# Turning the key-value sums over DRAM instead of on TensorE, normalising both query heads on ScalarE, and a new order of work

## The chip, the core and the metric

The kernel runs on one core of one Trainium2 chip. A core has five engines that run side by side and wait for each other by semaphores: TensorE (PE in the profile; PEld is its loading of weights), VectorE (DVE), ScalarE (ACT), GpSimd (POOL), and SyncE (SP), which here only issues DMAs. The time is that of one execution on the device in microseconds. A version is judged by the median of several runs; for the kernel before that is 1006.31 us over three runs, which lie between 1004.87 and 1006.49 us.

## The reference

Two stages. First linear attention over 8 batches of 8 heads, 576 tokens a batch, head size D = 64, with M = 128 random features:

```
phi(x) = exp(h - max(h)) / sqrt(M),  h = x @ omega.T - sum(x*x)/2      (x scaled by D**-0.25)
kv  = sum over s of phi(k)[s, m] * v[s, d]        # per batch and head: M x D
z   = sum over s of phi(k)[s, m]                  # per batch and head: M
out = (phi(q) @ kv) / (phi(q) @ z + 1e-6)
```

Then, over all 4608 tokens with the 8 heads side by side (512 columns), a feed-forward layer: `h = x @ w_in` (512 by 2048), `g = h - tanh(h)`, `g @ w_out` (2048 by 512). All inputs and the output are float32.

## The kernel before

**Precision by pieces.** TensorE works on float32r operands here. Where a product has to be better than one such pass, an operand is split into a high part (the cast) and a low part (the difference), and the product is the sum of two or three matmuls. ScalarE makes the high parts, VectorE (or GpSimd) the low ones.

**Units.** Work is cut into units, each with short steps. `f{ch}{f}` is one of 9 x 16 feed-forward units: token chunk `ch` (512 tokens) and block `f` (128 of the 2048 columns). Its steps are `h0` to `h3` (12 matmuls of 512 columns, L945), `th` (tanh on ScalarE, L974), `g` (VectorE, L975), `gh` and `gl` (high part on ScalarE, L963; low part on VectorE, L977), and `o0` to `o3` (12 matmuls, L970 to L972). `k{b}{c}` holds the keys and values of batch `b` and head pair `c`; `q{ch}{c}` the queries of chunk `ch` and head pair `c`. The first two batches and the first chunk use simpler native units (`k0*`, `k1*`, `n**`), and the weights are decoded during the first 120 us or so (`d*`).

**A query unit.** Features are made in `phi_q` (projection, L690, L695, exponent L701). VectorE forms the denominators (L732) and their reciprocals (L737, step `rc`). Steps `n0` and `n1` multiply the features of the two heads by them: `QN = "VA"` puts head 0 on VectorE in one instruction (L742) and head 1 on ScalarE in four (L745). Step `z` turns the features in blocks of 32 by 32 on VectorE (L750), step `s` writes them to DRAM with four DMAs (L756), step `r` reads them back into the layout that TensorE wants (L760). Steps `a`, `l`, `m` split them (L770, L774) and multiply them by the key-value sums (L780, L781); `ta` and `tv` bring the result to `xs` (L784, L788).

**A key unit.** Its matmuls (L852) gather in one PSUM bank, `pk`, for both heads: on the 128 partitions lie the 64 columns of the values' high parts and the 64 of their low parts, and along the row the 128 features, once for the keys' high and once for their low parts. Step `ca` (ScalarE, L879) and `cv` (VectorE, L882) add the two key parts into `c`, a tile of 128 x 2 heads x 128. Then step `kt` works on TensorE: two transposes of 128 x 128 (L886), one for each head, and one matmul that spreads the sums `z` over all partitions (L887). After that the value parts lie side by side; `ka` copies one of them (ScalarE, L892) and `kb` adds the other (VectorE, L895), which gives `kvt`; `zb` copies the spread `z` (L899); `wa` and `wv` split `kvt` into the operand `kvw` (L904, L907) that the query units use. The sums `z` themselves are made on GpSimd (L859, L860, L864) in a small tile `zs`, which is a part of `zf` (columns 14 and 15), and folded on VectorE (L867).

**Order.** The order of all steps is written out by hand in the string `ORDER`, some 4,900 words such as `k51.kt` or `f46.h0.5` (unit, step, and PSUM bank or buffer). The program issues the steps in this order, each to its own engine; every engine works off its instructions strictly in that order, and waits where an operand isn't ready. So an instruction that waits holds back everything behind it on its engine. The DMAs of SP form one such queue too. Matmuls of the feed-forward units fill TensorE while the attention units pass through the other engines.

Of the kernel before, what the change touches and what calls it, by code (L numbers as in the profile page):

```python
# [1088 lines left out]
```

## Time and profile before

| | us |
|---|---|
| median of three runs (lowest to highest) | 1006.31 (1004.87 to 1006.49) |
| the profiled execution, its own time | 1005.32 |
| span in its profile, first to last instruction | 1003.5 |
| TensorE busy | 986.4 (98% of the span) |
| VectorE busy | 802.9 (80%) |
| ScalarE busy | 683.4 (68%) |
| GpSimd busy | 325.3 (32%) |

A row of a group of instructions has the line, the engine and operation, what is written and read, the shape, the count, the busy time, the mean duration of one, and the idle time of the engine just before them with what ended it. Matmuls overlap: one may start while another is still running through, so the step from start to start tells what one costs in a row of them, and the duration of one doesn't. A wait row says who waited for whom, the sum in us, how often, and the longest.

### The profile page before, as it was taken

The numbers are of one execution on the slowest core, as the hardware profiler recorded it, in microseconds if no ns is written. First come the engines' busy times: TensorE is split into PE (matmuls) and PEld (weight loads), VectorE is DVE, ScalarE is ACT, GpSimd is POOL, SyncE is SP. The second block draws the span as 40 slices with busy tenths as digits, with TensorE's granted clock in tenths as the row PEclk, the third lists the DMA queues.
The fourth block names the chain that finished last, engine by engine and source line by source line (L and its number), as shares of the span: only waits on it lengthen the run. The fifth ranks groups of instructions, "written<-read, shape, count | busy, mean of one in ns | idle before, by whom it ended". The sixth has DMA issues, their size and how long they took to land.

```text
span 1003.5 us, 16665 instructions
## 1 busy us (share of the span) xinstructions
PE 986.4 (98%) x5024; PEld 817.8 (81%) x5024; DVE 802.9 (80%) x2698; ACT 683.4 (68%) x1677; POOL 325.3 (32%) x561
## 2 busy tenths in 40 slices
PE   9999999999999999999999999999999999999998
PEld 8688778888788788888888877888888888888886
DVE  7899868888888998988889999889999866744222
ACT  7878877677775787777767787687777675643222
POOL 2334314434334436343353434453623410001000
PEclk9899999999999999999999999999999999999999
DMA  9944731222302331312423222314222223110001
GB/s 356 374 165 77 178 88 56 82 82 65 108 20 80 99 108 57 101 53 75 129 56 98 77 86 71 101 30 117 66 77 71 69 85 105 32 54 32 1 10 43
DMA packets 45034, 91.15 MB, mean 91 GB/s; under 512 B 4880, under 2 KB 21648, under 8 KB 42896
## 3 DMA queue, kind: packets, MB, share of 16 engines
q1 hardware_dynamic: 43072, 84.12, 26.7%
q0 software_dynamic: 1584, 5.77, 3.0%
q8 instruction: 40, 0.66, 0.3%
q14 instruction: 50, 0.41, 0.1%
q10 hardware_dynamic: 288, 0.20, 0.1%
HBM read 60.18 MB, written 24.12 MB: 84 GB/s over the span
## 4 chain that ended last, share of the span: by engine, by line
PE 74%; DVE 14%; ACT 5%; DMA 3%; issue 2%; SPq 0%; POOL 0%; ACTq 0%; DVEq 0%; POOLq 0%
PE h L945 31%; PE po L970 10%; PE po L972 10%; PE po L971 10%; PE pj_q L684 2%; PE pk_k L852 2%; PE pn_q L781 1%; DMA phi_q<-qd_q 1%; DVE zf L975 1%; DVE zr L977 1%; DVE zf L732 1%; DVE qq_q L774 1%; PE pn_q L780 1%; DMA w<-a 1%; PE pj_k_B L684 1%
## 5 line engine op out<-in xcount | busy, mean ns | idle before, releaser
L945 PE MATMUL h<-xa,w 128*128 128x512 f32 x1728 | 439.6, 391 | 2.7 <-DMA w<-a 1.7
L945 PEld LDWEIGHTS h<-xa,w 128*128 128x128 f32 x1728 | 317.4, 188 | 68.7 <-DMA w<-a 2.1
L970 PE MATMUL po<-w,zr 128*128 128x512 f32 x576 | 226.8, 394 | 0.1
L972 PE MATMUL po<-w,zr 128*128 128x512 f32 x576 | 224.9, 390 | 0.3 <-DVE zr L977 0.3
L971 PE MATMUL po<-w,zr 128*128 128x512 f32 x576 | 224.8, 390 | 0.0
L977 DVE TENSOR_TENSOR zr<-zf,zr 128x512 fp32r<-128x512 f32 x144 | 103.1, 716 | 63.6 <-ACT zr L963 62.0
L963 ACT CAST zr<-zf 128x512 fp32r<-128x512 f32 x144 | 89.5, 621 | 88.5 <-PE po L971 48.3
L974 ACT ACTIVATE zf<-h 128x512 f32<-128x512 f32 x144 | 85.9, 597 | 76.2 <-PE h L945 49.8
L975 DVE TENSOR_TENSOR zf<-h,zf 128x512 f32<-128x512 f32 x144 | 98.7, 685 | 48.8 <-ACT zf L974 47.3
L972 PEld LDWEIGHTS po<-w,zr 128*128 128x128 f32 x576 | 108.1, 188 | 24.8 <-DVE zr L977 1.1
L970 PEld LDWEIGHTS po<-w,zr 128*128 128x128 f32 x576 | 108.2, 188 | 22.0 <-issue 1.3
L971 PEld LDWEIGHTS po<-w,zr 128*128 128x128 f32 x576 | 108.2, 188 | 19.1
L701 ACT ACTIVATE phi_q<-phi_q,nb_q 128x128 f32<-128x128 f32 x224 | 76.1, 397 | 4.2 <-DVE nb_q L695 3.9
L932 POOL TENSOR_TENSOR xa<-xs,xa 128x512 fp32r<-128x512 f32 x16 | 23.0, 1441 | 168.4 <-DVE xs L788 103.9
L824 POOL TENSOR_TENSOR khl_k_A<-phi_Ak,khl_k_A 128x256 fp32r<-128x256 f32 x48 | 38.8, 811 | 106.6 <-DVE khl_k_A L820 104.4
L732 DVE CUSTOM_DVE_ANT_0 zf<-phi_q,zb_k 128x128 bf16<-128x128 f32 (+1 forms) x240 | 63.4, 300 | 2.7 <-ACT zb_k L899 0.8
L695 DVE CUSTOM_DVE_ANT_0 phi_q<-pj_q,phi_q 128x128 f32<-128x128 f32 x224 | 54.5, 283 | 8.9 <-ACT phi_q L690 8.4
L774 DVE TENSOR_TENSOR qq_q<-phi_q,qq_q 128x512 fp32r<-128x512 f32 x56 | 41.6, 743 | 20.0 <-ACT qq_q L770 19.7
L824 POOL TENSOR_TENSOR khl_k_B<-phi_Bk,khl_k_B 128x256 fp32r<-128x256 f32 x48 | 38.9, 816 | 41.0 <-DVE khl_k_B L820 37.4
L690 ACT COPY phi_q<-pj_q 128x256 f32<-128x256 f32 x112 | 39.4, 370 | 18.8 <-PE pj_q L684 18.2
L770 ACT CAST qq_q<-phi_q 128x512 fp32r<-128x512 f32 x56 | 34.6, 617 | 22.6 <-PE pn_q L781 11.9
L684 PE MATMUL pj_q<-om,x_q 128*128 128x256 f32 x224 | 42.4, 288 | 1.8 <-DVE xs L788 0.9
(151 smaller groups left out, 1686.9 us busy)
## 6 DMA issues: line engine op xcount, KB each, us to landing
raw<-w SPq DMA_DIRECT2D x16, 1024.0 KB, 9.3
qd_q<-tq_q SPq DMA_DIRECT2D x112, 128.0 KB, 2.4
phi_q<-qd_q SPq DMA_DIRECT2D x28, 512.0 KB, 3.4
out<-zf SPq DMA_DIRECT2D x35, 256.0 KB, 2.0
f_q<-qT SPq DMA_DIRECT2D x28, 256.0 KB, 3.0
v_k<-vt SPq DMA_DIRECT2D x24, 288.0 KB, 2.8
f_k<-kT SPq DMA_DIRECT2D x24, 288.0 KB, 3.2
w<-a POOLq DMA_DIRECT2D x11, 512.0 KB, 4.6
```

The source lines that it names most:

```text
L684: nc.tensor.matmul(v["pj"][:, i], x, om2, start=True, stop=True)
L701: nc.scalar.activation(u[kind][:, at + i], u[kind][:, at + i], AF.Exp, bias=v["nb"][:, i : i + 1], scale=-1.0)
L732: nc.vector.tensor_tensor_reduce(next(turn)[r], u["ph"][r, i], kvs[b, c][1][r, h], scale=1.0, scalar=EPS, op0=ALU.mult, op1=ALU.add, accum ...
L824: nc.gpsimd.tensor_sub(k[:, :m, 1], u["ph" + g[0]][:, t : t + m], k[:, :m, 0].bitcast(F32))
L945: nc.tensor.matmul(u["p"], w_, x[:, c], start=(c, i) == (0, 0), stop=(c, i) == (NC - 1, 2))
L963: nc.scalar.copy(u["gh"], g)
L970: nc.tensor.matmul(po, gh, whi, start=f == 0, stop=False)
L971: nc.tensor.matmul(po, gh, wlo, start=False, stop=False)
L972: nc.tensor.matmul(po, gl, whi, start=False, stop=f == NF - 1)
L974: st = dict(th=lambda: nc.scalar.activation(g, blocks(u["p"]), AF.Tanh), g=lambda: nc.vector.tensor_sub(g, blocks(u["p"]), g), gh=g_hi, gl ...
L975: g=lambda: nc.vector.tensor_sub(g, blocks(u["p"]), g),
L977: gl=lambda: nc.vector.tensor_sub(u["gl"], g, u["gh"].bitcast(F32)))
```

## The change

In the key unit the two transposes on TensorE, the copy `ka` and the addition `kb` are gone. In their place VectorE folds the lower 64 partitions of `c` onto the upper 64 (`cf`), turns the 64 x 256 result in blocks of 32 by 32 (`ct`), writing into `zs`; SP writes it to DRAM with two DMAs (`cs`), and reads it back into `kvt` with one (`kb`, now a DMA). `kt` keeps the matmul for `z` alone. `wa` and `wv` read and write the same elements in another pattern. `QN` becomes `"AA"`: ScalarE normalises both heads, with eight instructions, and VectorE none. The string `ORDER` is new as a whole.

```diff
-QN = "VA"
+QN = "AA"
...
-k51.zh.1 k51.ca f46.h2 k52.vhA0.0 f45.gh.1 k51.cv k51.zl f46.h3 q51.e3 q50.r f45.gl q51.e2 k51.kt f47.h0.2 k52.sv1
-k51.zb f46.th f47.h1 q51.d3 k51.ka k51.kb f47.h2 q51.d2 k51.wa f47.h3 k52.vlA0 q51.rc q50.a0 k52.vlA1 f45.o0 f46.g
...
+k51.kt f46.h3 k51.zb k51.cf f47.h0.5 k51.ct f46.th q51.d2 k51.cs f47.h1 f46.g s3.d2 f47.h2 k52.vlA0 f46.gh.0 f47.h3
+q51.d3 k52.vlA1 q50.a0 q51.rc f48.h0.6 f46.gl q51.n1 f48.h1 q50.l0 k51.kb f45.o0 k52.tA0 q51.n0 k52.sv1 q50.m0.7 f45.o1
+q50.ta0 q51.z f45.o2 k52.eA0 f48.h2 k51.wa q52.sv k52.cA1 q51.s f47.th f46.o0 f45.o3 f47.g f48.h3 q53.ld k52.khA0.0
...
-        def turned():
-            for h in range(2):
-                nc.tensor.transpose(u["pk"][:, 0, h], u["c"][:, h], ident)
+        def c_fold():
+            nc.vector.tensor_add(u["c"][0:D], u["c"][0:D], u["c"][D:P])
+
+        def c_turned():
+            nc.vector.transpose(zs[0:D].rearrange("p h m -> p (h m)").rearrange("p (j h c) -> p h j c", j=4, h=2),
+                                u["c"][0:D].rearrange("p h (j c) -> p h j c", c=32))
+
+        def c_scatter():
+            d = u["d"] = dr.tile([4, 32, 2, D], F32, tag="cd", name=f"cd_{n}", bufs=2)
+            for i in range(2):
+                nc.sync.dma_start(d[:, :, i].rearrange("j r x -> r j x"),
+                                  zs[32 * i : 32 * i + 32].rearrange("p h m -> p (h m)").rearrange("p (j x) -> p j x", j=4))
+
+        def c_gather():
+            y = ak.tile([P, 2, 2, 32], F32, tag="kvt", name=f"kvt_{n}")
+            nc.sync.dma_start(y.rearrange("p i h c -> p (i h c)"), u["d"].rearrange("j r i x -> (j r) (i x)"))
+            u["kvt"] = y.rearrange("p i h c -> p h i c")
+
+        def z_all():
             nc.tensor.matmul(u["pk"][:, 1].rearrange("p h m -> p (h m)"), ones[:, 0:1].to_broadcast([P, P]),
                              u["zhl"][:, 0].rearrange("p h m -> p (h m)"), start=True, stop=True)
-
-        def kv_hi():
-            u["kvt"] = ak.tile([P, 2, D], F32, tag="kvt", name=f"kvt_{n}")
-            nc.scalar.copy(u["kvt"], u["pk"][:, 0, :, D:])
-
-        def kv_sum():
-            nc.vector.tensor_add(u["kvt"], u["pk"][:, 0, :, 0:D], u["kvt"])
...
+        def w_part(s):
+            return u["w"][:, s, :].rearrange("p h (i c) -> p h i c", c=32)
+
         def w_hi():
             u["w"] = sb.tile([P, 4, D], F32R, tag=f"kvw{b % 2}{c}", name=f"kvw_{n}")
-            nc.scalar.copy(u["w"][:, 0::3, :], u["kvt"])
+            nc.scalar.copy(w_part(slice(0, 4, 3)), u["kvt"])
 
         def w_lo():
-            nc.vector.tensor_sub(u["w"][:, 1:3, :], u["kvt"], u["w"][:, 0::3, :].bitcast(F32))
+            nc.vector.tensor_sub(w_part(slice(1, 3)), u["kvt"], w_part(slice(0, 4, 3)).bitcast(F32))
```

How the new order moves instructions is shown at the end of one key unit, batch 5 and head pair 1 (`k5_1`). TensorE before, from the last matmuls of that unit's sums on; `pk_k5_1` is its PSUM bank, `pj_k5_2` the projection of the next key unit, `h_4_6` and `po_4_0` feed-forward work:

```order
L852 MATMUL pk_k5_1_6135<-khl_k5_1_B0_6234,vhl_k5_1_B0_6191 128x256 x2
L852 MATMUL pk_k5_1_6135<-khl_k5_1_B1_6275,vhl_k5_1_B1_6198 128x256 x2
L684 MATMUL pj_k5_2_A0_6311<-om_93,x_k5_2_6256 128x256 x2
L945 MATMUL h_4_6_6292<-xa_98,w6_951 128x512 x6
L886 MATMUL pk_k5_1_6135<-zf_70,c1_k5_1_6316 128x128 x2
L887 MATMUL pk_k5_1_6135<-zhl_k5_1_6314,ones_96 128x256
L945 MATMUL h_4_7_6338<-xa_98,w7_917 128x512 x12
```

And TensorE now, around the same unit's matmul for `z`:

```order
L985 MATMUL po_4_3_6103<-w4_871,zr_69 128x512
L986 MATMUL po_4_3_6103<-w4_871,zr_69 128x512
L987 MATMUL po_4_3_6103<-w4_871,zr_69 128x512
L687 MATMUL pj_k5_2_A1_6396<-om_93,x_k5_2_6323 128x256 x2
L906 MATMUL pk_k5_1_6177<-zhl_k5_1_6378,ones_96 128x256
L960 MATMUL h_4_6_6334<-xa_98,w6_956 128x512 x3
L960 MATMUL h_4_7_6407<-xa_98,w7_924 128x512 x12
```

The two transposes are gone; the matmul for `z` remains, and feed-forward work follows it as before.

ScalarE before, from the copy `zb` of that unit past its cast `wa` (`kvw_k5_1`); `dn_q5_1` marks the normalising of the query unit of chunk 5 and head pair 1:

```order
L899 COPY zb_k5_1_6343<-pk_k5_1_6135 128x256
L974 ACTIVATE zf_70<-h_4_6_6292 128x512
L892 COPY kvt_k5_1_6351<-pk_k5_1_6135 128x128
L904 CAST kvw_k5_1_6361<-kvt_k5_1_6351 128x2x64
L770 CAST qq_q5_0_0_6368<-phi_q5_0_5854 128x512
L745 ACTIVATE phi_q5_1_6133<-phi_q5_1_6133,dn_q5_1_6212 128x128 x4
L963 CAST zr_69<-zf_70 128x512
```

And ScalarE now, the same stretch:

```order
L911 COPY zb_k5_1_6404<-pk_k5_1_6177 128x256
L989 ACTIVATE zf_70<-h_4_6_6334 128x512
L978 CAST zr_69<-zf_70 128x512
L773 CAST qq_q5_0_0_6436<-phi_q5_0_5871 128x512
L748 ACTIVATE phi_q5_1_6191<-phi_q5_1_6191,dn_q5_1_6250 128x128 x8
L787 COPY xs_99<-pn_q5_0_0_6465 64x512
L704 ACTIVATE phi_Ak5_2_6384<-phi_Ak5_2_6384,nb_k5_2_A0_6457 128x128 x2
L919 CAST kvw_k5_1_6485<-kvt_k5_1_6452 128x2x64
L693 COPY phi_Ak5_2_6384<-pj_k5_2_A1_6396 128x256
L989 ACTIVATE zf_70<-h_4_7_6407 128x512
L978 CAST zr_69<-zf_70 128x512
```

The copy into `kvt` is gone, the normalising has eight instructions in place of four, and the cast `wa` stands seven rows behind `zb` instead of three, with a projection's copy, a feed-forward tanh and a feed-forward cast right behind it.

SP now, around the same unit; `cd` is the DRAM buffer of the key-value sums, `qd` that of the queries, `f_` and `v_` are loads:

```order
L897 DMA cd_k5_1_6417<-zf_70 32x4x64 x2
L1026 DMA out<-zf_70 128x512
L902 DMA kvt_k5_1_6452<-cd_k5_1_6417 128x128
L759 DMA qd_q5_1_6490<-tq_q5_1_6474 32x4x256 x4
L716 DMA f_q5_3_6506<-qT 128x512
L810 DMA f_k5_3_6511<-kT 128x576
L763 DMA phi_q5_1_6191<-qd_q5_1_6490 128x1024
```

And SP before, in the same place, where the key unit issues nothing:

```order
L811 DMA v_k5_1_6012<-vt 128x576
L713 DMA f_q5_2_6042<-qT 128x512
L811 DMA v_k5_2_6237<-vt 128x576
L756 DMA qd_q5_0_6277<-tq_q5_0_6259 32x4x256 x4
L760 DMA phi_q5_0_5854<-qd_q5_0_6277 128x1024
L756 DMA qd_q5_1_6413<-tq_q5_1_6402 32x4x256 x4
```

Three DMAs of the key unit now stand in SP's queue; the read-back waits there for the two writes to land, and the queries' scatter stands behind it.

## Rows read from the trace of the kernel before

**Rows 1.** The page's list of engines: busy time, share of the span, instructions.

```profile
PE 986.4 (98%) x5024; PEld 817.8 (81%) x5024; DVE 802.9 (80%) x2698; ACT 683.4 (68%) x1677; POOL 325.3 (32%) x561
```

**Rows 2.** Busy time of each engine in five stretches of the span (us from its start: length, then busy time and instructions of each engine, the granted TensorE clock, the DMA share, GB/s).

```profile
0.00:120.00 120.00, 114.13 (x776) 92.55 (x776) 103.75 (x258) 97.57 (x229) 39.76 (x54) 0.97 0.73 241
120.00:300.00 180.00, 178.22 (x898) 146.97 (x898) 151.68 (x537) 130.11 (x328) 66.46 (x121) 1.00 0.25 69
300.00:800.00 500.00, 494.62 (x2460) 413.15 (x2458) 450.32 (x1649) 369.89 (x940) 212.59 (x383) 1.00 0.28 82
800.00:950.00 150.00, 150.00 (x678) 124.63 (x677) 82.97 (x235) 73.25 (x160) 6.54 (x4) 1.00 0.17 52
950.00:1003.50 53.50, 49.41 (x218) 40.53 (x217) 14.18 (x21) 12.54 (x21) 0.00 (x0) 0.99 0.07 25
```

**Rows 3.** TensorE's instructions in order of time, in a row of feed-forward matmuls and where one key unit ends (start, length, engine, line, operation, count).

```profile
401.34 2.88 PE L945 MATMUL h<-xa,w 128*128 128x512 f32 x12
404.06 0.52 PE L684 MATMUL pj_q<-om,x_q 128*128 128x256 f32 x3
...
415.98 0.40 PE L684 MATMUL pj_k_A<-om,x_k 128*128 128x256 f32 x2
416.22 0.38 PE L886 MATMUL pk_k<-zf,c_k 128*128 128x128 f32 x2
416.36 0.36 PE L887 MATMUL pk_k<-zhl_k,ones 128*128 128x256 f32 x1
416.56 0.40 PE L684 MATMUL pj_k_A<-om,x_k 128*128 128x256 f32 x2
```

**Rows 4.** The page's chain of work that ended last, by engine.

```profile
PE 74%; DVE 14%; ACT 5%; DMA 3%; issue 2%; SPq 0%; POOL 0%; ACTq 0%; DVEq 0%; POOLq 0%
```

**Rows 5.** Groups of instructions by line and shape: those that go, those that come more often, and those that stand nearest to the new ones.

```profile
L886 PE MATMUL pk_k<-zf,c_k 128*128 128x128 f32 x48 | 9.1, 271 | 0.0
L886 PEld LDWEIGHTS pk_k<-zf,c_k 128*128 128x128 f32 x48 | 6.4, 139 | 2.5 <-DVE c_k L882 0.2
L892 ACT COPY kvt_k<-pk_k 128x128 f32<-128x128 f32 x24 | 6.5, 269 | 2.1 <-PE pk_k L887 2.1
L895 DVE TENSOR_TENSOR kvt_k<-pk_k,kvt_k 128x128 f32<-128x128 f32 x24 | 6.8, 285 | 0.2
L867 DVE TENSOR_TENSOR zf<-zf 64x256 f32<-64x256 f32 x24 | 10.7, 446 | 2.9 <-POOL zf L864 2.2
L872 DVE CAST zhl_k<-zf 64x256 fp32r<-64x256 f32 x24 | 6.8, 282 | 1.6 <-PE pk_k L852 1.0
L750 DVE STREAM_TRANSPOSE tq_q<-phi_q 128x512 f32<-128x512 f32 x56 | 36.4, 688 | 0.5
L742 DVE TENSOR_TENSOR phi_q<-phi_q,dn_q 128x512 f32<-128x512 f32 x28 | 20.0, 714 | 0.4
L745 ACT ACTIVATE phi_q<-phi_q,dn_q 128x128 f32<-128x128 f32 x112 | 35.8, 391 | 10.6 <-DVE dn_q L737 10.6
```

**Rows 6.** DMAs that the query units send over DRAM: the page's list of issues (count, KB each, median us from issue to landing), and the lengths of the issues on SP (least, median, longest in ns).

```profile
qd_q<-tq_q SPq DMA_DIRECT2D x112, 128.0 KB, 2.4
phi_q<-qd_q SPq DMA_DIRECT2D x28, 512.0 KB, 3.4
L756 SPq DMA_DIRECT2D qd_q<-tq_q x112: 303/437/459, 182.2 to 879.7; - x112
L760 SPq DMA_DIRECT2D phi_q<-qd_q x28: 320/338/338, 186.2 to 882.2; - x28
```

**Rows 7.** Who waited for whom: what ScalarE waited for from those DMAs, and ScalarE's two longest waits in sum.

```profile
ACT qq_q L770 <- DMA qd_q<-tq_q: 5.6, 4, 2.1
ACT qq_q L770 <- DMA phi_q<-qd_q: 4.8, 7, 1.1
ACT zf L974 <- PE h L945: 49.8, 39, 4.4
ACT zr L963 <- PE po L971: 48.3, 20, 6.0
```

**Rows 8.** The same for TensorE, its two longest waits in sum, and for SP's queue, the longest in sum.

```profile
PE h L945 <- DMA w<-a: 1.7, 1, 1.7
PE pn_q L781 <- DVE qq_q L774: 1.4, 4, 0.7
SPq L756 <- DVE tq_q L750: 171.9, 19, 20.3
```

More of the change, by code (lines that the diff above doesn't have):

```diff
@@ new lines @@
+k43.ct k43.cs f3f.h0.7 q50.sa q43.z f3f.h1 s2.d2 k51.ld f3d.gh.1 f3c.o1 q43.s f3d.gl f3f.h2 q50.sv f3f.h3 f3e.th x4.h1
+f3c.o2 k50.lv q42.ta1 f3c.o3 f3e.g q51.ld x4.h0 k43.kb q42.tv1 f3d.o0 f3e.gh.0 x4.l0 f3d.o1 x4.h2 q43.r f3e.gl f3d.o2
+x4.l1 f3f.th k50.pA0.6 k50.vhM.1 k50.pA1.3 k50.cA0 k50.pM.0 f3e.o0 k43.wa k50.cM k50.vhA0.0 k50.cA1 f3e.o1 k50.tM x4.l2
+f3f.g f3e.o2 k50.tA1 q43.a0 k43.wv f3d.o3 k50.tA0 k50.eA1 q43.l0 f3e.o3 f3f.gh.1 k50.vlA0 q50.p0.0.0 q43.m0.7 k50.eA0
+f3f.gl f40.h0.3 q43.a1 k50.khA0.0 k50.klA0 f3f.o0 q50.c0 q43.l1 q43.ta0 f3f.o1 k50.zA s3.c0.1 q43.tv0 q50.p2.6 s3.d0
@@ new lines @@
+q43.m1.4 q50.c2 s3.c1.0 k50.kvA0.7 q43.ta1 f3f.o2 k50.khA1.1 k50.vhA1.0 s3.d1 q43.tv1 f3f.o3 k50.klA1 q50.t0 x4.h3
+f40.h1 k50.vlA1 k50.vlM q50.e0 q50.p3.1 x4.l3 k50.pB0.4 q50.c3 k50.pB1.0 k50.eM k50.kvA1 f40.h2 k50.cB0 k50.cB1 q50.d0
+f40.h3 s3.c2.1 k50.khM.0 s3.c3.0 f41.h0.5 k50.klM f40.th k50.tB0 k50.vhB0.0 s3.d3 k50.kvM k51.sa f40.g q50.p1.2
+k50.vhB1.1 f41.h1 k50.tB1 f41.h2 f40.gh.0 k51.sv0 f41.h3 k50.eB0 f40.gl f42.h0.4 q50.c1 q51.sa k50.khB0.1 k51.sv1 f42.h1
+k50.klB0 f42.h2 k50.vlB0 k50.eB1 f42.h3 f41.th k50.khB1.0 k50.zB q50.t1 f40.o0.3 q50.t3 f40.o1.0 f41.g k50.klB1 q50.t2
@@ new lines @@
+f40.o2.2 f41.gh.1 k50.vlB1 k50.zM k51.pA0.1 k51.lv f41.gl k50.kvB0 k51.cA0 k50.kvB1 k52.ld k51.pA1.5 f43.h0.6 k51.tA0
+k51.cA1 f42.th k50.zf f41.o0 k50.ca k50.zh.1 q50.e1 f42.g f41.o1 k50.zl q50.e2 k50.cv f43.h1 q51.sv k51.vhA0.0 q50.e3
+f40.o3.1 k51.vhA1.1 f41.o2 f42.gh.0 k50.cf f43.h2 k51.eA0 f42.gl k51.pM.4 k50.kt f43.h3 k51.vlA0 k50.zb k51.khA0.0
+k51.cM k50.ct f42.o0 k51.klA0 f43.th k51.tA1 k50.cs k51.tM f42.o1 k51.vlA1 k51.eM q50.d2 q52.ld k51.eA1 f42.o2 q50.d3
+f44.h0.7 k51.khA1.1 q50.d1 f41.o3 f43.g k51.kvA0.5 k50.kb k51.zA q51.p0.4.1 q51.p1.6 q51.c0 f44.h1 f43.gh.1 q51.t0
@@ new lines @@
+k51.klA1 f44.h2 q51.c1 k51.khM.0 q51.e0 k51.vhM.0 f44.h3 f43.gl q51.t1 f42.o3 f44.th q50.rc k51.klM k51.pB0.4 f44.g
+k51.pB1.6 k51.cB0 k51.kvA1 k50.wa f43.o0 k51.tB0 k51.cB1 k51.vhB0.1 f44.gh.0 q51.d0 f45.h0.7 k51.eB0 k51.vlM f45.h1
+k51.vlB0 q51.e1 k50.wv k51.tB1 f45.h2 q50.n0 f44.gl k51.kvM q51.p2.4 k51.khB0.1 k51.vhB1.0 q51.d1 q51.p3.6 q51.c2 f44.o0
+k51.klB0 k51.eB1 f43.o1 q51.c3 k51.zB q50.n1 q51.t3 f44.o1 k51.vlB1 f43.o2 k52.lv k52.sa q50.z k51.zM f45.h3 f46.h0.6
+f45.th f43.o3 k51.khB1.0 q52.sa q50.s f44.o2 k52.sv0 k51.klB1 f46.h1 f45.g k51.kvB0 k51.zf f45.gh.1 k52.pA0.7 k52.vhA0.1
@@ new lines @@
+q51.t2 k51.kvB1 f46.h2 k51.zh.1 k51.ca k52.vhA1.0 k52.cA0 k51.cv k51.zl f44.o3 q51.e2 f45.gl q51.e3 k52.pA1.4 q50.r
+k51.kt f46.h3 k51.zb k51.cf f47.h0.5 k51.ct f46.th q51.d2 k51.cs f47.h1 f46.g s3.d2 f47.h2 k52.vlA0 f46.gh.0 f47.h3
+q51.d3 k52.vlA1 q50.a0 q51.rc f48.h0.6 f46.gl q51.n1 f48.h1 q50.l0 k51.kb f45.o0 k52.tA0 q51.n0 k52.sv1 q50.m0.7 f45.o1
+q50.ta0 q51.z f45.o2 k52.eA0 f48.h2 k51.wa q52.sv k52.cA1 q51.s f47.th f46.o0 f45.o3 f47.g f48.h3 q53.ld k52.khA0.0
+f47.gh.1 k53.ld k51.wv k52.klA0 f46.o1 k52.tA1 f47.gl k52.eA1 f46.o2 k52.khA1.1 k52.kvA0.5 k52.zA f48.th q50.tv0
@@ L921, in k_unit @@
             st["kv" + g] = partial(kv, g=g)
-        st.update(zA=partial(zsum, 0), zB=partial(zsum, 1), zM=z_mid, zf=z_fold, zh=z_hi, zl=z_lo, ca=c_hi, cv=c_sum, kt=turned,
-                  ka=kv_hi, kb=kv_sum, zb=zb, wa=w_hi, wv=w_lo)
+        st.update(zA=partial(zsum, 0), zB=partial(zsum, 1), zM=z_mid, zf=z_fold, zh=z_hi, zl=z_lo, ca=c_hi, cv=c_sum, cf=c_fold, ct=c_turned, cs=c_scatter,
+                  kb=c_gather, kt=z_all, zb=zb, wa=w_hi, wv=w_lo)
         return st
```

622 lines of the change are left out of this document (301 added, 321 removed).

## The prediction

> **What bounds the kernel now.** I read the list of engines first: TensorE is busy for 986.4 of 1003.5 us, VectorE for 80%, ScalarE for 68% [rows 1]. The stretches come next, because an average hides the stage: from 300 to 800 us TensorE has 494.6 of 500 us, VectorE 450.3, ScalarE 369.9; from 800 to 950 us TensorE is never idle, and the others are half free [rows 2]. The granted clock is 1.00 from 120 to 950 us, which is the upper of its two levels. So TensorE sets the pace, and VectorE, at 90%, is the helper with the least room. TensorE's idle time is 5.9 us up to 120, then 1.8, 5.4 and 0.0 up to 950, and 4.1 at the end [rows 2]; its longest wait in sum is one of 1.7 us, the next 1.4 us in four [rows 8]. Busy time is not all work at full pace, since matmuls overlap and their ends are modelled, so short stalls can hide in it; I allow as much again as the 7.2 us that show between 120 and 950. The chain of work that ended last gives TensorE 74% and VectorE 14% [rows 4]: on most of the way a microsecond of matmuls is a microsecond of time, on a quarter of it another engine hands on.
>
> **The change part by part.** All terms are held against the profiled execution, 1005.3 us by its own clock, of which 1003.5 us are its span; it is 1.0 us below the median of 1006.31, inside the spread of the runs.
>
> *The transposes go from TensorE.* The two of one unit start at 416.22 us and the next matmul at 416.36 us, without a gap: 0.14 us for a unit, though the row gives each 271 ns of length [rows 3, 5]. With 24 units that is 3.4 us. Lower bound: only the chain's TensorE share counts, 74% of it, 2.5 us [rows 4]. Upper bound: if the loading of their weights is what really holds the array, 6.4 us [rows 5]. I take 3.3 us, a touch under the full sum, because the start-to-start step is the nearest row and TensorE isn't idle before any of them (0.0 in the row).
>
> The Trainium skill weighs this choice the other way: "VectorE: DVE Perf Modes", section "Rules for kernel authors", says to do a 128 x 128 transpose on TensorE where a PSUM destination will do, and to use VectorE for 32 x 32 blocks. By that rule the step would stay, and the 3.3 us with it. The row decides here, I think, because the rule compares lengths of one operation and this kernel is short of TensorE steps.
>
> *VectorE.* It loses 28 multiplications of 714 ns (20.0 us) and 24 additions (6.8 us). It gains 24 folds of 64 x 256, the form of L867 with 446 ns, 10.7 us, and 24 block transposes of 64 x 256 [rows 5]. The trace has none of that size; L750 takes 688 ns for twice the row, and L872 reads and writes a 64 x 256 tile in 282 ns, so it lies between 6.8 and 16.5 us in sum; I take 350 ns, half of L750, 8.4 us. Net: 7.7 us less (0 to 9).
>
> *ScalarE.* It loses 24 copies (6.5 us) and gains 112 multiplications, at L745's busy time of 35.8 us for as many: 29.3 us more, nearly all from 180 to 880 us. That lifts it from 74% to some 78% there, still under VectorE's 89%. By itself this costs nothing: its two longest waits, 98 us in sum, are for TensorE [rows 7], and in that time the extra work fits. The cover would be gone where a normalising of 8 x 0.32 = 2.6 us stands ahead of a tanh or cast that TensorE wants next; if that held TensorE for 1 us in one of four units, it would be 7 us, the upper bound; the lower is 0. The new order keeps more work between the reciprocal and the turning than before, so I take 0.
>
> *The DRAM trip.* Two writes issue for 0.44 us each and land after 2.4 us, the read issues for 0.34 us and lands after 3.4 us, if they behave as those of the queries [rows 6]: 7.0 us from the end of `ct` until `wa` may run, and 7.4 us with `ct` itself, where before it took two short instructions. In unit `k51` the order puts nine feed-forward steps of three matmuls and one of four short ones between `ct` and `wa`; twelve such matmuls start within 2.72 us, 0.227 each, and two of 256 columns within 0.24 [rows 3]: 27 x 0.227 + 4 x 0.12 = 6.6 us. So there ScalarE stands at `wa` for about 0.8 us, and behind `wa` wait a projection's copy, a tanh and a cast. Counted in the same way over all 24 units, nine have under 7.6 us and the rest 8 to 17 us. Some 9 x 0.6 = 5 us of ScalarE waits, then; before, it waited 10.4 us in eleven places for the queries' DMAs [rows 7], and none of TensorE's longest waits names one. I cost it at nothing on TensorE; bounds are nothing and the whole 5 us.
>
> "DMA: Bandwidth & Descriptors" in the Trainium skill, section "Specifications", puts full rate at transfers of 512 B and up, with a read-modify-write below. The runs written here are 256 B long (64 floats), those of the queries 1 KB. If by that the writes took twice the queries' 2.4 us, all of the nine units and three or four more would wait, by 2.4 us longer; that is the slower rival below. No row of the kernel before shows a data DMA with such short runs.
>
> *SP's queue.* It gets 24 x (2 x 0.44 + 0.34) = 29 us of issues, and waits at each read for the writes, about 2.4 us. Behind it stand the queries' scatter and loads. SP spends 171.9 us in front of the queries' scatter, waiting for the turned features [rows 8], so it has the time. Nothing; at most those 2.4 us for a load in a unit or two.
>
> *Buffers.* The turned sums lie in `zs` until the writes have landed, so GpSimd can't start the next unit's sums before that; in the order the next one stands 2.8 us or more behind, and GpSimd is idle for more than half of each stretch [rows 2]. The PSUM bank `pk` comes free after `zb` instead of after `kb`, somewhat earlier. Both at nothing. `wa` and `wv` handle the same number of elements: nothing.
>
> *The new order.* It can give back at most the idle time that shows from 120 to 950 us, 7.2 us, and about as much that doesn't show; it can take as much. In the first 120 us, where weights stream at 241 GB/s, it may shift either way by a few of the 5.9 us. The distances between a feed-forward unit's last split and the matmuls that use it have grown on average, those of the queries have shrunk. I take 1 us of gain, for VectorE's 7.7 us, and the bounds as -8 and +8.
>
> **Sum.** 1005.3 - 3.3 - 1.0 = 1001.0 us for a run like the profiled one, and 1002.0 beside the median; I forecast 1001.5 us.
>
> **The rivals.**
> *More comes back than was taken.* With VectorE relieved and room in the order, the stalls of 120 to 950 us, seen and hidden, fall by half, about 7 us more: 994 us. For it: the wait of TensorE that comes back most often is one for VectorE [rows 8]. Against: the order's distances are mixed.
> *It is paid back.* The 3.3 us of steps go, and feed-forward matmuls come to wait for ScalarE's 29 us of new work instead, one in eight of the 28 normalisings by 1 us: 1005 to 1006 us. For it: ScalarE must make two of the four helpers' steps of each feed-forward unit. Against: its 26% of idle time.
> *The trip over DRAM is late: slower.* Place: `wa` on ScalarE. If the path is 2.4 us longer than I reckon, some 13 units wait 1.5 us on average beyond the 5 us above, and the other eleven none: 25 us of ScalarE, of which TensorE loses what its buffers don't cover, a third to a half, 8 to 12 us: 1010 to 1014 us, taken as 1011. It decides from the point where TensorE loses more than 3.3 us, a wait of about 0.5 us in each unit at a third. For it: runs a quarter as long as the queries', and a read that waits in SP's queue behind an output DMA in `k51`. Against: the queries make the same trip.
> That the change doesn't do what it says is excluded: the order has no transpose left in those 24 places.
>
> **How the numbers follow.** Forecast (998 to 1004 us) 0.45; more comes back 0.22; paid back 0.21; slower 0.12. A measurement of this kernel tells 0.2%, 2 us, from no change: faster is below 1004.3 us, 0.45 + 0.22 = 0.67; within, 0.21; slower, above 1008.3 us, 0.12. The range from 993.5 to 1008 us leaves out the slow case and a third of the first rival, about 0.2.
>
> **What would show it.** No TensorE group for the transposes, and the matmul for `z` as it was. ScalarE near 713 us busy, VectorE near 795. The waits of `wa` for the read-back in some ten places, under 1 us each; 2 us or more in most units means the slow rival. TensorE's idle time from 120 to 950 us near 7 us: 3 or less speaks for the first rival, 12 or more against the forecast. The block transpose near 350 ns, the writes landing after 2.4 us. I am wrong if the time falls by much more than 3.3 us while TensorE's stalls stay as they are.

## The result and the profile after

The changed kernel takes 1011.25 us (median of 20 runs, 1008.1 to 1021.04); the kernel before, run beside it on the same chips, takes 1006.27 us (20 runs). The ratio is 1.0067, with a 95% interval from 1.005 to 1.0083: slower, by 5.0 us in the medians and about 6.7 us by the ratio, where 4 to 5 us of gain were forecast. The profiled execution took 1010.64 us, its span is 1008.9 us. Four executions of the later runs, three at a granted clock of about 0.85 and one of 3419 us, are left out of the medians and ratios below.

The list of engines of the kernel after, against [rows 1]:

```profile
PE 983.1 (97%) x4976; PEld 813.4 (81%) x4976; DVE 790.3 (78%) x2694; ACT 711.7 (71%) x1765; POOL 322.6 (32%) x561
```

TensorE has 3.3 us less, VectorE 12.6 us less, ScalarE 28.3 us more: near what was reckoned, VectorE even below it. The stretches, with the columns of [rows 2]:

```profile
0.00:120.00 120.00, 110.03 (x755) 89.17 (x756) 101.84 (x239) 94.07 (x218) 35.34 (x47) 0.96 0.70 232
120.00:300.00 180.00, 177.48 (x890) 146.15 (x889) 151.10 (x546) 136.37 (x344) 70.47 (x125) 1.00 0.29 79
300.00:800.00 500.00, 490.57 (x2413) 408.32 (x2412) 439.32 (x1645) 387.36 (x1002) 209.67 (x384) 1.00 0.30 85
800.00:950.00 150.00, 150.00 (x682) 124.53 (x681) 83.36 (x246) 80.73 (x182) 7.08 (x7) 1.00 0.20 58
950.00:1008.90 58.90, 55.05 (x243) 45.26 (x242) 14.70 (x22) 13.16 (x22) 0.00 (x0) 1.00 0.05 19
```

TensorE's idle time is 10.0, 2.5, 9.4, 0.0 and 3.9 us. Against [rows 2] that is 4.1 us more at the start, 4.8 us more from 120 to 950 us and 0.2 us less at the end; with 3.3 us less busy time it makes the 5.4 us by which the span grew. The clock is at its upper level from 120 us on. So no work was added that TensorE has to do: it waits, 8.6 us more. For what, the waits say (sum in us, times, longest); against [rows 7, 8]:

```profile
ACT zr L978 <- PE po L986: 52.8, 28, 4.6
...
ACT zf L989 <- PE h L960: 41.5, 38, 3.7
...
ACT kvw_k L919 <- DMA kvt_k<-cd_k: 3.3, 5, 1.0
PE h L960 <- DMA w<-a: 3.1, 1, 3.1
...
PE pn_q L784 <- DVE qq_q L777: 2.3, 6, 0.7
PE pn_q L783 <- ACT qq_q L773: 2.3, 4, 1.0
PE n_pn L604 <- ACT n_qt L597: 1.9, 2, 1.4
...
PE pn_q L783 <- DVE nb_k_B L698: 1.6, 2, 1.0
```

ScalarE still waits for TensorE most of all, 94 us in the first two rows, where it was 98. The trip over DRAM (third row) holds it up for 3.3 us in five places, and no wait of TensorE names that trip. Of TensorE's rows, the one for weights (`w<-a`, 1.7 us in [rows 8]) and the one of the native units (`n_pn`) belong to the start. The other three stand in front of the query units' numerators (`pn_q`), which wait for their splits `a` and `l`, or for what VectorE has to do ahead of them. The chain by engine, against [rows 4], gives VectorE less and ScalarE and the DMAs more:

```profile
PE 74%; DVE 11%; ACT 7%; DMA 5%; issue 2%; SPq 1%; POOL 0%; DVEq 0%; ACTq 0%; POOLq 0%
```

The groups of the changed work, against [rows 5]:

```profile
L906 PE MATMUL pk_k<-zhl_k,ones 128*128 128x256 f32 x24 | 7.4, 307 | 0.5 <-POOL zhl_k L878 0.4
L888 DVE TENSOR_TENSOR c_k<-c_k 64x256 f32<-64x256 f32 x24 | 10.2, 423 | 0.7
L891 DVE STREAM_TRANSPOSE zf<-c_k 64x256 f32<-64x256 f32 x24 | 10.3, 429 | 0.7
L748 ACT ACTIVATE phi_q<-phi_q,dn_q 128x128 f32<-128x128 f32 x224 | 69.5, 390 | 11.3 <-DVE dn_q L740 11.0
```

The DMAs over DRAM (count, KB each, median us from issue to landing), against [rows 6]; `cd` and `kvt` are the new ones:

```profile
qd_q<-tq_q SPq DMA_DIRECT2D x112, 128.0 KB, 2.4
cd_k<-zf SPq DMA_DIRECT2D x48, 32.0 KB, 1.6
kvt_k<-cd_k SPq DMA_DIRECT2D x24, 64.0 KB, 2.3
```

TensorE around one unit's matmul for `z` (start, length), against the lower part of [rows 3]:

```profile
418.64 0.40 PE L687 MATMUL pj_k_A<-om,x_k 128*128 128x256 f32 x2
418.87 0.28 PE L906 MATMUL pk_k<-zhl_k,ones 128*128 128x256 f32 x1
418.99 0.40 PE L985 MATMUL po<-w,zr 128*128 128x512 f32 x1
```

From the start of the `z` matmul to the next start it is now 0.12 us. Before it was 0.34 us for the two transposes and that matmul together (416.22 to 416.56 us, [rows 3]): not only the transposes went, the matmul behind them became shorter too. In 17 of the 24 units its step is now 0.12 us, in the other seven 0.16 to 0.23 us. Added up over the 24 units in the two traces, these steps go from 8.2 to 3.5 us: 4.7 us are gone.

### The profile page after: what moved, and what is told of

It reads as the page before. It is cut to its first block, busy times and chain, and to the rows that moved or that the text cites. A ratio compares the mean times of both kernels' runs of the same rounds, so it can differ in the third digit from the quotient of the medians.

```text
span 1008.9 us, 16796 instructions
## 1 busy us (share of the span) xinstructions
PE 983.1 (97%) x4976; PEld 813.4 (81%) x4976; DVE 790.3 (78%) x2694; ACT 711.7 (71%) x1765; POOL 322.6 (32%) x561
## 3 DMA queue, kind: packets, MB, share of 16 engines
q1 hardware_dynamic: 53440, 87.27, 28.3%
## 4 chain that ended last, share of the span: by engine, by line
PE 74%; DVE 11%; ACT 7%; DMA 5%; issue 2%; SPq 1%; POOL 0%; DVEq 0%; ACTq 0%; POOLq 0%
PE h L960 32%; PE po L985 10%; PE po L986 10%; PE po L987 10%; PE pj_q L687 2%; PE pk_k L855 2%; DMA phi_q<-qd_q 2%; ACT phi_q L748 1%; DVE zf L735 1%; DMA w<-a 1%; PE pn_q L784 1%; DMA qd_q<-tq_q 1%; PE pn_q L783 1%; DVE zf L990 1%; PE pj_k_B L687 1%
## 5 line engine op out<-in xcount | busy, mean ns | idle before, releaser
L960 PE MATMUL h<-xa,w 128*128 128x512 f32 x1728 | 444.1, 393 | 4.5 <-DMA w<-a 3.1
L748 ACT ACTIVATE phi_q<-phi_q,dn_q 128x128 f32<-128x128 f32 x224 | 69.5, 390 | 11.3 <-DVE dn_q L740 11.0
L827 POOL TENSOR_TENSOR khl_k_B<-phi_Bk,khl_k_B 128x256 fp32r<-128x256 f32 x48 | 42.8, 894 | 38.3 <-DVE khl_k_B L823 38.0
```

Of the source, the lines that this page charges most:

```text
L748: nc.scalar.mul(ph[:, t], ph[:, t], rd[:, t : t + 1])
L827: nc.gpsimd.tensor_sub(k[:, :m, 1], u["ph" + g[0]][:, t : t + m], k[:, :m, 0].bitcast(F32))
L960: nc.tensor.matmul(u["p"], w_, x[:, c], start=(c, i) == (0, 0), stop=(c, i) == (NC - 1, 2))
```

## The experiments

Eighteen versions ran, numbered in the order in which they ran; each was compared with the kernel before on the same chip. "Old" and "new order" are the strings `ORDER` of before and after. What was measured, as ratio to the kernel before with its 95% interval:

| run | order | work | median us | ratio |
|---|---|---|---|---|
| changed kernel | new | both edits | 1011.25 | 1.0067 (1.0050 to 1.0083) |
| 1 | new | DRAM trip, `QN = "VA"` | 1017.90 | 1.0121 (1.0089 to 1.0152) |
| 2 | old | transposes, `QN = "AA"` | 1020.76 | 1.0141 (1.0114 to 1.0168) |
| 3 | old start, new rest | both edits | 1008.39 | 1.0021 (1.0001 to 1.0041) |
| 4 | old | DRAM trip, `"VA"` | 1028.39 | 1.0223 (1.0193 to 1.0252) |
| 5 | new start, old rest | as in the kernel before | 1006.15 | 1.0016 (0.9996 to 1.0036) |
| 6 | new, 56 numerators later | both edits | 1073.41 | 1.0674 (1.0649 to 1.0699) |
| 7 | as 6, old start | both edits | 1071.13 | 1.0651 (1.0626 to 1.0676) |
| 8 | new | transposes, `"AA"` | 1013.38 | 1.0084 (1.0060 to 1.0108) |
| 9 | new | both, head 0 not normalised | 1009.84 | 1.0046 (1.0029 to 1.0062) |
| 10 | old | as in the kernel before, head 0 not normalised | 1001.86 | 0.9967 (0.9955 to 0.9979) |
| 11 | old, trip earlier | DRAM trip, `"VA"` | 1028.46 | 1.0233 (1.0211 to 1.0254) |
| 12 | new | both, head 0 on GpSimd | 1012.28 | 1.0070 (1.0055 to 1.0086) |
| 13 | new, nine numerators later | both edits | 1013.27 | 1.0088 (1.0064 to 1.0113) |
| 14 | as 13, old start | both edits | 1010.82 | 1.0056 (1.0038 to 1.0073) |
| 15 | new | both, without `cf` and `ct` | 1003.60 | 0.9994 (0.9972 to 1.0015) |
| 16 | new | as 15, and head 0 not normalised | 1001.54 | 0.9959 (0.9944 to 0.9973) |
| 17 | old | as in the kernel before, head 0 on GpSimd | 1005.56 | 1.0004 (0.9992 to 1.0015) |
| 18 | new | as in the kernel before | 1017.84 | 1.0153 (1.0119 to 1.0187) |

**Each edit without the other, in either order (runs 1, 2, 4, 8, 18).** Runs 1 and 2 change one line each; run 4 keeps the old order and puts the new steps into it (`wa` some 8 us behind `ct`); run 8 takes the new order and puts the old steps back (`ka` and `kb` where `cf` and `ct` stood); run 18 is run 8 with `"VA"`. The diffs show one place of 24.

```diff
 run 1 (run 2 the other way)
-QN = "AA"
+QN = "VA"
 run 4
-k51.ka k51.kb f47.h2 q51.d2 k51.wa f47.h3
+k51.cf k51.ct k51.cs f47.h2 q51.d2 f47.h3
 run 8
-k51.cf f47.h0.5 k51.ct f46.th q51.d2 k51.cs f47.h1
+k51.ka k51.kb f47.h0.5 f46.th q51.d2 f47.h1
```

> The changed kernel with QN back at VA: VectorE normalises head 0 again, nothing else differs. Theory O (the new order of work costs the time, at the start and where the numerators stand close behind their splits; the edits themselves gain some 3 us): within 3 us of the changed kernel, about 1011 us. Theory A (ScalarE's 28 us of extra work holds up TensorE): 4 to 8 us faster than the changed kernel, 1003 to 1007 us. Theory D (the trip over DRAM holds up ScalarE): about 1011 us, as in O.

> The kernel before with QN at AA alone: old order, transposes on TensorE, ScalarE normalises both heads. Theory A: 4 to 8 us slower than before, 1010 to 1014 us. Theories O and D: within 3 us of before, 1004 to 1009 us.

> The old order with the key-value sums turned over DRAM and QN at VA: the fold, the block transpose and the writes stand where the copy of the old key unit stood, the read-back some 1.5 us of matmuls later, the cast wa about 8 us of matmuls behind the block transpose. Theory O: the edit shows its own gain, 2 to 6 us under before, 1000 to 1004 us. Theory D: the trip costs more than the transposes did, 1008 us or more. Theory A: as O, since ScalarE keeps its old work.

> The new order and QN at AA with the old key unit: transposes on TensorE, copy ka and addition kb placed up to 1.4 us of matmuls behind the copy zb, no trip over DRAM. If the trip over DRAM saves what TensorE's steps say (5.4 us: the z matmul has become 0.08 us shorter too): 4 to 8 us slower than the changed kernel, 1015 to 1019 us. If the trip (theory D) is what holds the changed kernel up: faster than it, 1008 us or less.

> The work of the kernel before, unchanged (two transposes on TensorE, ka, kb, head 0 normalised on VectorE), in the new order; where cf and ct stood, ka and kb stand, as in the run with the transposes. It fills the missing corner: the order alone. Theory O (the order is the loss, the edits gain in it): the gains of the two edits in the new order add, 5.4 us for ScalarE's normalising (1.0121 to 1.0067) and 1.7 us for the trip over DRAM (1.0084 to 1.0067), so 1.0067 + 0.0054 + 0.0017 = 1.0138, 1017 to 1022 us. Rival (the edits are the loss, the order is at most the start): 1006 to 1010 us.

In the new order ScalarE's normalising helps: with the old work the order stands at 1.0153, with the normalising at 1.0084, with both edits at 1.0067. The last step, the trip over DRAM, is within the intervals (so is 1.0153 to 1.0121); the normalising (also 1.0121 to 1.0067) is not. In the old order the same edits cost 1.4% and 2.2%. By the ratios, the new order with the old work in it is 15 us slower than the old one (12 to 19 us; 12.4 us by the medians), and the edits bring back 8.6 us. The times of runs 1, 2 and 8 lie outside every range given for them: all those ranges took order and edits for things that add up, and they don't. No run has the old order with both edits, so the loss can be divided between order and edits only along the way that was measured. The stretches of run 18 show the loss in the same places:

```profile
0.00:120.00 120.00, 110.60 (x768) 89.39 (x769) 105.41 (x246) 95.39 (x221) 37.84 (x52) 0.99 0.70 234
120.00:300.00 180.00, 177.71 (x896) 146.19 (x895) 150.47 (x546) 132.61 (x335) 68.39 (x121) 1.00 0.28 75
300.00:800.00 500.00, 489.59 (x2414) 405.27 (x2413) 436.84 (x1630) 367.46 (x936) 206.38 (x377) 1.00 0.28 80
```

TensorE idles 9.4 us at the start and 12.7 us up to 800 us, although the sums don't go over DRAM there and ScalarE has no extra work. A part of that belongs to where run 18 puts the old steps: TensorE waits for `kb` there, which it doesn't in the kernel before. The largest such row, and three smaller ones, make 3.4 us:

```profile
PE h L951 <- DVE kvt_k L901: 2.1, 7, 0.5
```

How an order fits one set of work is seen in run 2. In the old order VectorE stands 26.4 us in front of the turning of the queries' features, waiting for ScalarE's normalising; in the new order the same wait is 6.5 us (run 2 first, then the changed kernel):

```profile
DVE tq_q L750 <- ACT phi_q L745: 26.4, 26, 2.3
DVE tq_q L753 <- ACT phi_q L748: 6.5, 11, 1.5
```

In run 4 TensorE's longest waits are for GpSimd's low parts in front of the key sums, and for the queries' splits; GpSimd in turn waits for the turned sums to land in DRAM:

```profile
PE pk_k L860 <- POOL khl_k_A L832: 5.8, 3, 2.1
PE pn_q L789 <- DVE qq_q L782: 3.4, 11, 0.5
POOL zf L868 <- DMA cd_k<-zf: 6.5, 5, 2.3
```

Run 11 sent the sums to DRAM right behind `cv` in the old order because of that last row; the time stayed (1.0223 and 1.0233). So the landing hardly explains run 4, and what it loses by stays open.

```diff
-k51.cv k51.zl f46.h3 ... k51.cf k51.ct k51.cs
+k51.cv k51.zl k51.cf k51.ct k51.cs f46.h3 ...
```

> The old order with the trip over DRAM and QN at VA, as in the run of that kind, but with the fold, the block transpose and the writes right behind the addition of the key parts, so that the writes have landed earlier before GpSimd needs the shared tile for the next unit's sums. If GpSimd's wait for that tile caused a good part of the 23 us lost there (TensorE waited 11 us for the key units' sums): 5 to 12 us faster than that run, 1016 to 1023 us. If it was the delayed cast or VectorE's extra 12 us: within 3 us of it.

**The start (runs 3 and 5).** The words of the first part (weights, native units, feed-forward units of chunk 0) were exchanged between the two orders, all others left where they stood; the diff shows a few of those words.

```diff
 run 3 (run 5 the other way)
-f00.g d3.hi f01.h3 k12.kvf d5.v1 f02.h0.6 f00.gh.0 d3.lo
+f00.g d3.hi f01.h2 k12.kvf d5.v1 f01.h3 f00.gh.0 d7.v1
```

> The changed kernel with the first part of the order (native units, decoding, feed-forward units of chunk 0) taken from the kernel before, with PSUM banks renamed to fit; the rest of the order stays new. Theory O: the 4 us that TensorE was idle longer in the first 120 us come back, about 1007 us. Theories A and D: the start has no part in it, 1011 us.

> The kernel before with the first part of the order (native units, decoding, feed-forward units of chunk 0) taken from the changed kernel, PSUM banks renamed to fit; the mirror of the run with the old first part. If the new first part costs some 3 us by itself: 3 to 5 us slower than before, about 1009 us. If the 3 us of that run were chance or belong to the join: within 1.5 us of before.

By the ratios, the old start takes 4.6 us from the changed kernel (1.0067 to 1.0021), which leaves it 0.1 to 4.1 us behind the kernel before. The new start costs the old rest 1.6 us, which can't be told from nothing. The first 120 us of run 3, then of run 5:

```profile
0.00:120.00 120.00, 113.75 (x773) 92.10 (x774) 103.44 (x258) 96.90 (x228) 38.90 (x54) 0.96 0.73 239
0.00:120.00 120.00, 110.74 (x771) 89.72 (x772) 105.57 (x249) 96.10 (x224) 38.57 (x53) 1.00 0.70 234
```

In run 3 TensorE is idle for 6.3 us there, close to the 5.9 us of [rows 2], its wait for weights is 1.8 us again, and the wait of the native units is gone. In run 5 it is idle for 9.3 us, but the granted clock of the stretch is 1.00, where it is 0.97 in the kernel before, so the two differ in more than the order, and the price of the start in front of the old rest stays open. In front of the new rest it makes 4.6 of the 6.7 us, by the ratios.

**The numerators (runs 6, 7, 13, 14).** In runs 6 and 7 all 56 numerators stand 1.3 us later; in runs 13 and 14 only nine, in front of which TensorE waits in the profiles of the new order.

```diff
 run 6
-k50.vlA0 q50.p0.0.0 q43.m0.7 k50.eA0 f3f.gl f40.h0.3 q43.a1 k50.khA0.0 k50.klA0 f3f.o0 q50.c0
+k50.vlA0 q50.p0.0.0 k50.eA0 f3f.gl f40.h0.3 q43.a1 k50.khA0.0 k50.klA0 f3f.o0 q43.m0.7 q50.c0
 run 13
-q50.p0.0.0 q43.m0.7 k50.eA0 f3f.gl f40.h0.3 q43.a1
+q50.p0.0.0 k50.eA0 f3f.gl f40.h0.3 q43.m0.7 q43.a1
```

> The changed kernel with the numerators of the queries (steps m0, m1, and ta, tv where needed) moved later by about two feed-forward steps, 1.3 us of matmuls, in all 28 query units; nothing else. Theory N (in the new order the numerators stand too close behind their splits, so TensorE waits 11 us in front of them where it waited 6): 4 to 7 us faster than the changed kernel, 1004 to 1007 us. Theory A (ScalarE has too much to do, so that a wait taken away here comes back at another matmul): less than 2 us gained, 1009 us or more.

> The changed kernel; only the nine numerators that wait for their split in the profile of every version with the new order (q20.m1, q23.m1, q31.m0, q43.m0, q51.m0, q53.m0, q53.m1, q62.m1, q63.m0; 6.9 of 7.3 us of TensorE's idle time in front of numerators) are moved behind work of TensorE that stands next in the order and is ready: 0.5 to 0.9 us of feed-forward or projection matmuls each. Theory N (these numerators stand too close behind their splits, and that is the loss after 120 us): the waits fall to under 2 us, and the kernel takes 1004 to 1007 us, 4 to 7 us less than the changed kernel, so about the time of the kernel before. Rival R (the wait is only a symptom: the splits come late with the whole of VectorE and ScalarE, and a later numerator moves the wait to the next matmul, or to the copy out of it): 1009 to 1013 us, the idle time from 120 to 950 us stays near 12 us. Rival C (what happened with all 56 moved): slower, over 1015 us.

> As the run before, with the first part of the order taken from the kernel before. Theory S+N (the start and the nine numerators together are the whole loss, 4 us and 5 to 7 us): 1000 to 1003.5 us, faster than the kernel before by 0.2 to 0.6%, which is about what the removed transposes and the shorter z step are worth (5 us). Rival R: 1006 to 1009 us, as with the old first part alone. Rival C: over 1012 us.

Run 6 (and 7, the same with the old start) told only how little may be moved: ScalarE, which works strictly in order, then stands at the next splits and at the copies out of the numerators (5.1 and 8.1 us in the changed kernel).

```profile
ACT qq_q L778 <- PE pn_q L789: 40.0, 21, 4.5
ACT xs L792 <- PE pn_q L789: 34.7, 27, 2.8
```

Run 13 brought my theory down. The waits in front of numerators fell from 7.1 to 2.9 us, but others came in their place, TensorE's idle time from 120 to 950 us rose from 12.0 to 14.0 us, and the time stayed (1.0088, overlapping 1.0067). Its stretch from 300 to 800 us, and the waits:

```profile
300.00:800.00 500.00, 488.74 (x2394) 405.30 (x2393) 434.99 (x1636) 385.16 (x996) 208.32 (x380) 1.00 0.30 85
```

```profile
PE pk_k L860 <- POOL khl_k_A L832: 2.0, 3, 1.0
PE pj_k_B L692 <- DVE nb_k_M L703: 1.4, 1, 1.4
PE pn_q L788 <- ACT qq_q L778: 1.3, 3, 0.7
PE pk_k L911 <- POOL zhl_k L883: 1.3, 3, 0.7
```

Run 14, the same behind the old start, gained nothing either: 1.0056, where run 3 has 1.0021. A wait that moves on to another matmul when its own is put off is a symptom. That the helpers hand over late as a whole is the reading that fits; these two runs don't show it by themselves.

**The load of the helpers (runs 9, 10, 12, 15, 16, 17).** Runs 9, 10 and 16 leave step `n0` out of the order, runs 15 and 16 the steps `cf` and `ct`; runs 12 and 17 do `n0` on GpSimd.

```diff
 runs 9, 10, 16
-q51.n0
 runs 15, 16
-k51.cf
-k51.ct
 runs 12, 17 (QN is "AA" before 12, "VA" before 17)
+QN = "PA"
...
+elif QN[h] == "P":
+    for t in range(WB):
+        nc.gpsimd.tensor_scalar(ph[:, t], ph[:, t], rd[:, t : t + 1], 1.0, op0=ALU.mult, op1=ALU.mult)
```

> The changed kernel without the normalising of head 0 in the query units (112 ScalarE instructions left out, so half of the attention's division is not done); everything else as it is. Theory A (ScalarE's 36 us of extra normalising hold up TensorE): 5 us or more faster than the changed kernel, 1006 us or less, and TensorE's waits in front of the numerators fall from 11 to some 6 us. Theory O (the order itself is tight, whatever ScalarE carries): less than 3 us faster, 1008 us or more.

> The kernel before without the normalising of head 0 (28 VectorE instructions of 0.71 us left out, half of the attention's division not done). It tells what 20 us less on VectorE are worth in the old order. If the relief of VectorE is worth something there: 2 to 5 us faster than before, 1001 to 1004 us. If VectorE's load doesn't set the time: within 1.5 us of before.

> The changed kernel with the normalising of head 0 on GpSimd (four instructions of about 0.46 us in each unit) instead of ScalarE; order unchanged. Theory A: as without the normalising, 1003 to 1007 us, if GpSimd's own order isn't held up. Theory O: 1009 us or more.

> The changed kernel without the fold cf and the block transpose ct of the key units (what is written to DRAM are GpSimd's sums of features instead, so the key-value sums are left out of the output); 20.5 us less on VectorE, nothing else moved. Theory V (TensorE waits because VectorE hands over late, whatever stands behind it): as in the old order, where 20 us off VectorE were worth 4 us, and as in the new one, where 20 us more on it cost 5 us: 1004 to 1007 us here, TensorE's idle time from 120 to 950 us falls from 12 to 8 us or less. Theory P (the places in the order fix the waits, whatever the load): 1009 to 1011 us, the numerators' waits stay.

> As the run before, and without the normalising of head 0 of the query units on ScalarE too (half the division left out): VectorE then has 770 us and ScalarE 682, about what they have in the old order without head 0's normalising (783 and 683 us), which took 1001.9 us and still had the transposes. So the two compare the orders at the same load of the helpers. If the new order costs nothing by itself, this run lies 3 to 5 us below that one, at 997 to 999 us. If the order itself is the cost (theory O), it lies at 1003 to 1007 us, not below it.

> The kernel before, with its own order and the transposes on TensorE; only head 0 of the query units is normalised on GpSimd (four instructions of 492 ns as measured in the run with the new order) instead of VectorE (714 ns). VectorE has 20 us less, GpSimd 55 us more of its two thirds idle; the path from the reciprocal to the turned features gets 1.3 us longer. Theory V: 1002 to 1004.5 us, a gain of 2 to 4 us over the kernel before. Rival: the longer path or GpSimd's sums behind it hold up the key units: 1006 to 1015 us, as with ScalarE in that place (1020.8 us).

ScalarE's new work is worth 2.1 us (run 9) to 3.5 us (run 15 to 16), both with overlapping intervals, and moving it to GpSimd gives nothing. In the old order the same work on ScalarE is worth 17.5 us (run 2 to run 10). Twenty microseconds off VectorE are worth 3.3 us in the old order (run 10). In the new one they are worth 7.5 us when the same step `n0` goes (run 1 to run 9), and 7.3 us when `cf` and `ct` go (run 15); run 15 also shortens the way to the trip over DRAM, and ScalarE's wait at `wa` falls there from 3.3 to 1.3 us, so not all of its gain need be VectorE's load. Runs 10 and 16 compare the orders with `n0` left out of both; TensorE in the two, from 120 to 800 us, run 10 first:

```profile
120.00:300.00 180.00, 178.19 (x898) 146.83 (x897) 147.45 (x536) 130.40 (x328) 64.67 (x120) 1.00 0.26 70
300.00:800.00 500.00, 496.69 (x2482) 417.53 (x2481) 442.10 (x1636) 371.86 (x948) 211.76 (x384) 1.00 0.29 82
```

```profile
120.00:300.00 180.00, 178.13 (x893) 147.94 (x893) 148.15 (x543) 132.83 (x332) 68.76 (x121) 0.99 0.29 78
300.00:800.00 500.00, 493.69 (x2443) 413.05 (x2442) 429.07 (x1614) 368.15 (x929) 210.12 (x385) 1.00 0.31 85
```

Run 16 has 4.7 us fewer steps on TensorE and some 13 us less on VectorE from 300 to 800 us, and still idles 6.3 us there, where run 10 idles 3.3 us; in the first 120 us it idles 9.7 us, run 10 5.8 us. The two times can't be told apart, and run 16's 1001.5 us lies between the two ranges that were given for it. So even with lighter helpers the new order eats what the removed work gives, more than half of it at the start. Run 17 shows that VectorE's 20 us can't be had in the old order by handing them to GpSimd, whose instructions take 442 ns each there and 492 ns in run 12: there is no gain. No version here that does all the work is faster than the kernel before.

## Why the prediction was wrong

It said faster, with 1001.5 us; its range ended at 1008 us. By its own steps:

- **The transposes** were mis-sized, on the good side: 3.3 us were taken, the steps give 4.7 us, within the bounds. I had reckoned the `z` matmul "as it was"; its step fell from 0.20 to 0.12 us in most units. "VectorE: DVE Perf Modes" in the Trainium skill, section "Rules for kernel authors", would leave a 128 x 128 transpose on TensorE. Run 8 did so in the new order, and took 1.0084 against 1.0067, with overlapping intervals; in the old order, leaving the transposes there is better by 2.2% (run 4). So here the order decides.
- **VectorE**: 7.7 us less were reckoned, 12.6 us less are seen; by the rows of the edit it is 20.0 + 6.8 - 10.2 - 10.3 = 6.3 us, the block transpose taking 429 ns where I took 350; the other 6.3 us lie in instructions that the edit doesn't touch, and why they got shorter stays open. What a microsecond of VectorE is worth, I did not price. By runs 1, 9 and 10 it is 0.17 us of time in the old order and some 0.37 us in the new one.
- **ScalarE** was put at nothing, with 7 us as upper bound. Measured in the new order: 2 to 3.5 us, inside the bound.
- **The DRAM trip** was right. It is shorter than reckoned, 1.6 + 2.3 us of landing for 2.4 + 3.4, and holds ScalarE for 3.3 us in five places where I had 5 us in nine. The slower rival gave 1011 us, which is the time that came; but its mechanism, `wa` waiting for a late read, isn't there. The writes in runs of 256 B landed sooner than the queries' in runs of 1 KB (1.6 to 2.4 us, at a quarter of the bytes). "DMA: Bandwidth & Descriptors" in the Trainium skill, section "Specifications", puts full rate at 512 B and up. No run here writes as many bytes in longer runs, so the landing times can't tell what the short runs cost; the packets of 256 B in this trace take 20 ns in the median, those of 1 KB 60 ns, a third more per byte.
- **SP's queue and the buffers** cost nothing that shows: after the start no wait of TensorE names a load, and in the changed kernel GpSimd never waits for the sums to land.
- **The new order** is the step that failed: "I take 1 us of gain, for VectorE's 7.7 us, and the bounds as -8 and +8". In place of the gain TensorE's idle time grew by 8.6 us, 4.1 us of it at the start, for which I had "a few of the 5.9 us" either way; the old start gives back 4.6 us (run 3). With the old work in it the order costs 15 us (run 18), twice the upper bound. I judged it from mean distances between splits and matmuls, and set bounds of the same size both ways; an order that holds TensorE at 98% has more to lose than to win. And the sum adds the terms as if each had a price of its own, where the edits' prices change with the order: ScalarE's normalising costs 14 us in the old one (run 2) and gains 5 to 7 us in the new one (run 1 to the changed kernel, run 18 to run 8).
- The rival "It is paid back" is nearest in kind: the steps went, and TensorE's waits came. But it named ScalarE's work, and that is only 2 to 3.5 us of it.
- Of what was to show it, TensorE's idle time from 120 to 950 us decided: "12 or more speaks against the forecast"; it is 12.0 us, just at that mark.

What is shown: TensorE's added idle time lies in the start (4.1 us; run 3 gets back 4.6 us of time there) and between 120 and 800 us (4.8 us); ScalarE's normalising gains in the new order and loses in the old one; a lighter VectorE shrinks the loss; and putting off the nine numerators that wait doesn't. What stays open is which placings behind the start make the new order worse: no single wait stands for it, and the runs moved only the start and the numerators. Open too is what both edits would take in the old order. That an order with other spacing would have brought out the 8.6 us of the edits is argued, not shown.

## What to carry to other kernels

When a change brings edits and a new order together, price them apart: old work in the new order, new work in the old. Where one engine is busy at 98% and all engines work in order, an order fits one set of work: here each half without the other lost 1.4% to 2.2%, the whole 0.7%. So such prices don't add up, and the start of the program deserves a look of its own. Before believing a wait row, put off the matmul that waits: if the wait turns up at the next one, look for the engine that is late, and price that by leaving out some of its work.

## What had not been expected of the hardware

- A matmul of 256 columns behind two transposes took 0.20 us from start to start in all units but one, behind other matmuls 0.12 us in 17 of 24 units: removing an instruction from TensorE can save more than its own step.
- Small writes to DRAM (32 KB in runs of 256 B) landed after 1.6 us, and the read-back of 64 KB after 2.3 us.
- GpSimd scales a 128 x 128 tile by one value per partition in 492 ns (run 12) or 442 ns (run 17), ScalarE in 390 ns.
